# One pool of two-bank tiles for both phases of a hash-attention and gated feed-forward kernel

## The chip, the core and the metric

The kernel runs on one core of a Trainium2 chip. Its time is the device time in microseconds of one execution. Before the change, three runs gave a median of 914.16 us (913.9 to 914.45).

The engines are named as in the profile: PE multiplies matrices, DVE does elementwise work on vectors, ACT applies functions (exponential, sign, copy), POOL and SP mostly issue transfers. PE writes its results into PSUM, which is used here as eight banks of 512 float32 values per partition. DVE and ACT read them from there.

## The reference: what is computed

```python
# q, k, v: (4, 8, 768, 64); proj: (64, 6)
q_bits = (q @ proj > 0); k_bits = (k @ proj > 0)        # 6 bits each
mask = bucket(q_bits)[:, None] == bucket(k_bits)[None, :]
scores = where(mask, q @ k.T / 8, -1e9)
attn = exp(scores - max) ; attn = attn / (attn.sum(-1) + 1e-09)
x = (attn @ v) as (3072 tokens, 512)
g = x @ w_gate                                           # w_gate, w_val: (512, 1536)
out = (g * sigmoid(g) * (x @ w_val)) @ w_out             # w_out: (1536, 512)
```

The inputs of the second half are float64 values that the kernel takes as pairs of words.

## The kernel before, in words

**Attention.** Heads are taken two at a time: 4 batches x 4 head pairs make 16 pairs, the outer loop from L625. In a pair, queries lie in two halves of 384 (`HQ`) and keys in six chunks of 128 (`NCH`), so a pair has 12 units, one per half and chunk.

For a unit, `products` (L517) takes two PSUM banks, one for each head, and multiplies the float32 scores into them. `mark` (L521) adds a second product, of hash bits in bfloat16, which pushes pairs of different buckets far down. Then ACT takes the exponential of each head's bank on its own, into the weights `A` (L524). `attend` (L531) multiplies the weights of a unit by v into a bank per half of the queries. ACT copies that bank to `xT` at the end of each half (L549), with a small step for `e` after the first half (L548). A pair's 12 units of scores come first and its 12 `attend` steps after them.

`front` (L415) prepares a pair: the transposes of q and k (on PE for the first pair, in `start_first`, L453, and on DVE for the others) and the hash products (`hash_blocks`, L420), which go to a bank of their own. ACT takes their signs (L428). For k, DVE spreads them over the rows (`spread_k`, L434). In the first pair the order is written out at L478 to L488: units 0 to 2 are multiplied, the signs of k and q by halves are taken in between, and the marks follow.

DVE adds up the weights (`add`, L553). `total` (L572) lets PE sum them over partitions into a bank, and ACT copies the sums' row to SBUF (L581). SP then sends the row on, DVE inverts it (`invert`, L586), and `norm` (L600) scales `xT` one pair later. Inside the pair loop the order is: scores of 12 units, `total` of the pair before, the next pair's hash products (`prepare_pair`, L642), pieces of weights, `attend`.

All PSUM tiles of this phase come from one pool of eight single banks (L304). A new tile takes the slot that is released first, and waits for the last reader of what was in it.

**The gated block.** It opens a pool of four tiles of two banks each (L676), once the attention's pool is closed. Tokens are taken in three blocks of 1024. For each group of 128 hidden columns, `up` (L689) makes the gate and the value, each as a product `a` of two parts of a split number and a product `n` of a third part. ACT and DVE join them into `hid`, whose third part comes last (L742). After each three groups an output part follows (L749): eight chunks of 128 tokens, a two-bank tile each, the first bank with the products of the parts h and l (`first` in `start`, L755), the second bank with those of the third part (`second`). In the last part of each block, four chunks are begun ahead with the groups that are ready (`ahead`, L797). DVE adds a finished tile to the output (`end`, L773, with L785 and L789, or L777 ahead of L785).

The very last chunk (`last`, L800) uses two tiles: one for the third part's product, one whose two banks take the two halves of the output columns. After each half DVE adds it (L813) and SP sends it out (L816).

**Loads.** The first q goes out from SP and the first k from ACT (L350), each in two halves of chunks. The first v follows on SP (L353). Later SP gets k, q and v of the second pair (L408) and the first weight words. The SP queue is worked in order.

Every instruction waits for its inputs and for the release of the tile it writes. There is no scheduler: the order on each engine is the program's own.

## Time and profile before

| what | value |
|---|---|
| median of three runs | 914.16 us |
| the profiled execution, whole | 914.08 us |
| its span, first to last instruction | 912.0 us |
| PE busy | 904.2 us, 99% of the span |
| DVE busy | 667.2 us, 73% |
| ACT busy | 453.8 us, 50% |
| granted TensorE clock | 0.999 |
| `A<-sc` on ACT (L524), 128x384, 384 of them | 155.9 us |
| one head pair in full swing | 19.23 us |

The span is a little shorter than the device time, since something lies around it on both sides. A row of the profile names the line, the engine, the operation and its tiles (`out<-in`), then the number of instructions. The times are busy time, the mean of one, and the idle time of the engine just before. The busy share of PE says only that some matmul was running; where PE stood still is told by its waits.

### The profile page before, as it was taken

What the parts mean: (1) busy time and instruction counts of PE and PEld (TensorE: products, weight loads), DVE (VectorE), ACT (ScalarE), POOL (GpSimd) and SP (SyncE); (2) the same over time, 40 slices, a digit from 0 to 9 for tenths busy, and PEclk for the clock granted to TensorE, in tenths of its full rate; (3) what the DMA queues carried; (4) which work ended last, traced back from release to release, by engine and by line L of the source; (5) the groups of instructions that cost most, each with busy time, mean ns of one, the idle gap of its engine ahead of it and who ended that gap; (6) DMA issues with size and microseconds to landing.
All of it is one profiled execution on the core that took longest, in us unless ns stands there. A gap on an engine that the chain in (4) does not pass through costs nothing.

```text
span 912.0 us, 12995 instructions
## 1 busy us (share of the span) xinstructions
PE 904.2 (99%) x4795; PEld 638.8 (70%) x4795; DVE 667.2 (73%) x774; ACT 453.8 (50%) x812; POOL 97.0 (11%) x193
## 2 busy tenths in 40 slices
PE   9999999999999999999999999999999999999997
PEld 5444444444444488888888788888888888888886
DVE  5999999998989768679776756464658754574746
ACT  6889888788887655452414133322313233313230
POOL 1011101010111210001000000101010100010000
PEclk9999999999999999999999999999999999999999
DMA  8677797778886699686756563434444642525232
GB/s 185 127 199 204 212 210 174 173 209 233 216 192 208 209 374 334 224 283 208 279 198 235 206 232 104 181 132 173 138 148 152 239 157 99 185 73 210 99 138 93
DMA packets 145582, 174.28 MB, mean 191 GB/s; under 512 B 106496, under 2 KB 115200, under 8 KB 145520
## 3 DMA queue, kind: packets, MB, share of 16 engines
q0 software_dynamic: 22864, 116.36, 36.4%
q1 hardware_dynamic: 121056, 56.71, 24.8%
q8 instruction: 38, 0.62, 0.3%
q10 hardware_dynamic: 1600, 0.39, 0.2%
q14 instruction: 24, 0.20, 0.1%
HBM read 133.17 MB, written 39.42 MB: 189 GB/s over the span
## 4 chain that ended last, share of the span: by engine, by line
PE 97%; DVE 2%; DMA 0%; ACTq 0%; ACT 0%; issue 0%; DVEq 0%
PE a L687 29%; PE o L687 20%; PE sc L514 17%; PE n L687 14%; PE av L539 14%; PE sum L578 1%; PE hps L423 1%; DMA kraw<-in_k_dram 0%; DVE hid L742 0%; DVE hid L740 0%; DVE v L732 0%; DVE v L736 0%; DVE xparts L292 0%; ACTq L329 0%; ACT hid L737 0%
## 5 line engine op out<-in xcount | busy, mean ns | idle before, releaser
L687 PE MATMUL a<-xparts,ring 128*128 128x512 f32 x1152 | 273.0, 389 | 0.6 <-ACT row L581 0.6
L687 PEld LDWEIGHTS a<-xparts,ring 128*128 128x128 f32 x1152 | 216.2, 188 | 46.2 <-ACT row L581 1.3
L687 PE MATMUL o<-ring,hid 128*128 128x512 f32 (+1 forms) x870 | 199.0, 388 | 2.3 <-DVE o L813 1.2
L687 PEld LDWEIGHTS o<-ring,hid 128*128 128x128 f32 x870 | 162.5, 188 | 37.2 <-DVE hid L742 2.4
L524 ACT ACTIVATE A<-sc 128x384 f32<-128x384 f32 x384 | 155.9, 504 | 8.1 <-PE sc L514 7.3
L514 PE MATMUL sc<-qT,kT 64*128 64x384 f32 x768 | 157.5, 488 | 0.0
L687 PE MATMUL n<-xparts,ring 128*128 128x512 f32 x576 | 142.3, 389 | 0.0
L539 PE MATMUL av<-A,vraw 128*64 128x386 f32 (+1 forms) x768 | 127.7, 488 | 0.0
L687 PEld LDWEIGHTS n<-xparts,ring 128*128 128x128 f32 x576 | 108.1, 188 | 22.4
L732 DVE TENSOR_TENSOR v<-v,n 128x1024 f32<-128x1024 f32 x36 | 44.0, 1221 | 99.4 <-PE n L687 98.8
L244 POOL DMA_DIRECT2D ring<-ram x108 | 56.9, 529 | 501.2 <-PE n L687 329.2
L539 PEld LDWEIGHTS av<-A,vraw 128*64 128x64 f32 x768 | 53.7, 137 | 73.3 <-issue 61.4
L514 PEld LDWEIGHTS sc<-qT,kT 64*128 64x128 f32 x768 | 70.3, 187 | 47.8 <-issue 41.9
L726 ACT ACTIVATE g<-a 128x1024 f32<-128x1024 f32 x36 | 36.9, 1026 | 132.1 <-PE a L687 127.2
L737 ACT ACTIVATE hid<-v 128x1024 fp32r<-128x1024 f32 x36 | 38.2, 1062 | 114.8 <-DVE v L736 114.8
L734 ACT ACTIVATE g<-g 128x1024 f32<-128x1024 f32 x36 | 38.2, 1061 | 85.2 <-DVE g L732 85.2
L789 DVE TENSOR_TENSOR o<-o 128x512 f32<-128x512 f32 x92 | 63.0, 687 | 20.6 <-ACT o L783 18.2
L732 DVE TENSOR_TENSOR g<-g,n 128x1024 f32<-128x1024 f32 x36 | 43.8, 1216 | 33.3 <-PE n L687 33.3
L514 PE MATMUL sc<-qb,kb 64*128 64x384 bf16 x384 | 66.0, 323 | 0.0
L560 DVE SCALAR_TENSOR_TENSOR both<-A 128x1536 f32<-128x1536 f32 x32 | 55.8, 1744 | 7.4 <-ACT A L524 6.1
L564 DVE TENSOR_TENSOR both<-both,A 128x1536 f32<-128x1536 f32 x32 | 56.2, 1757 | 3.2
L740 DVE SCALAR_TENSOR_TENSOR hid<-hid,v 128x1024 fp32r<-128x1024 f32 x36 | 44.0, 1223 | 19.2 <-ACT hid L737 19.1
(79 smaller groups left out, 701.0 us busy)
## 6 DMA issues: line engine op xcount, KB each, us to landing
ring<-ram POOLq DMA_DIRECT2D x108, 768.0 KB, 4.8
ram<-stage POOLq DMA_DIRECT2D x23, 768.0 KB, 5.6
ram<-stage SPq DMA_DIRECT2D x13, 768.0 KB
qraw<-in_q_dram SPq DMA_DIRECT2D x64, 96.0 KB
vraw<-in_v_dram SPq DMA_DIRECT2D x16, 384.0 KB
out_dram<-o SPq DMA_DIRECT2D x23, 256.0 KB
kraw<-in_k_dram SPq DMA_DIRECT2D x60, 96.0 KB
r<-sums SPq DMA_DIRECT2D x30, 192.0 KB
```

The lines of the kernel that those rows point to most:

```text
L244: nc.gpsimd.dma_start(t.bitcast(FP32), ram[at].bitcast(FP32))
L514: nc.tensor.matmul(banks_of[u][h], x["k", n][rows, ks], x["q", n][rows, qs], start=start, stop=not start)
L524: nc.scalar.activation(weights(u)[:, h, 0:HQ], sc, AF.Exp, scale=SCALE * (1.0 if units[u][0] else OFF / 2))
L539: nc.tensor.matmul(ps[h * D : (h + 1) * D, 0:width], raws["v", n][:, h, c, :], a[:, h, 0:width], start=c == 0, stop=c == NCH - 1)
L560: nc.vector.scalar_tensor_tensor(out=t, in0=first, scalar=S * EPS / P / 2, in1=now, op0=ALU.add, op1=ALU.add)
L564: nc.vector.tensor_tensor(t, t, now, op=ALU.add)
L687: nc.tensor.matmul(ps, w, x, start=start, stop=stop)
L732: nc.vector.tensor_tensor(two(z), two(z), n_, op=ALU.subtract)
L734: nc.scalar.activation(z, z, AF.Silu)
L737: nc.scalar.activation(h, val, AF.Copy, scale=TOWARD / STEP)
L740: nc.vector.scalar_tensor_tensor(out=l, in0=h.bitcast(FP32), scalar=-STEP, in1=val, op0=ALU.mult, op1=ALU.add)
L789: nc.vector.tensor_tensor(accs[c], accs[c], t[:, 1], op=ALU.subtract)
```

## The change

The change does five things.

1. One pool `pp` of four two-bank tiles is opened at the start and serves both phases; the pool of single banks and the second pool go. A unit's two heads share one tile, and one exponential of 128x2x384 takes both. Both halves of `attend` share a tile; `e` and one copy of 128x768 come at the end of the pair. The nine warm-up products go to one tile, and each first transpose takes one bank of a two-bank tile.
2. The hash products of pair n+1 and the sums of pair n-1 share a tile, `joint`. Its sums' row is copied after the hash products have been issued and after the two signs of q on ACT: `total` now returns the copying step as a function.
3. In the first pair the order of signs and marks changes: two signs, products 1 and 2, and then mark 0, sign of k's second half, mark 1, sign of q's second half, mark 2.
4. The first v is loaded after k and q of the second pair.
5. In the last output part of a block, the last group's first products of chunks 0 and 1 both come before the second product of chunk 0. The very last chunk takes three tiles, one for each half and one for the third part.

The diff, cut to its core:

```diff
--- before.py
+++ after.py
@@ -75,7 +75,11 @@
     RINGS = (3, 3)
     ringp = [ctx.enter_context(tc.tile_pool(name="ringp", bufs=RINGS[0]))]
     dram = ctx.enter_context(tc.tile_pool(name="dram", bufs=1, space=bass.MemoryType.DRAM))
+    pp = ctx.enter_context(tc.tile_pool(name="pp", bufs=4, space=PSUM))
     ctx.enter_context(tc.manual_schedule())
+
+    def two_banks(name):
+        return pp.tile([P, 2, 512], FP32, tag="pp", name=name)
 
     halves = [slice(half * HQ, (half + 1) * HQ) for half in range(2)]
 
@@ -301,10 +305,6 @@
         fixed = scope.enter_context(tc.tile_pool(name="fixed", bufs=1))
         att = scope.enter_context(tc.tile_pool(name="att", bufs=2))
         xp = scope.enter_context(tc.tile_pool(name="xp", bufs=4))
-        banks = scope.enter_context(tc.tile_pool(name="ps", bufs=8, space=PSUM))
-
-        def bank(name):
-            return banks.tile([P, 512], FP32, tag="ps", name=name)
 
         pairs = [(b, pr) for b in range(B) for pr in range(NP)]
         raws = {}
@@ -350,7 +350,6 @@
         for half in range(2):
             fetch(0, "q", nc.sync, half)
             fetch(0, "k", nc.scalar, half)
-        fetch(0, "v", nc.sync)
 
         ident = fixed.tile([P, P], FP32, tag="ident", name="ident")
         make_identity(nc, ident)
@@ -363,9 +362,9 @@
         nc.vector.memset(zeros, 0.0)
         for t in (sides["k", 0], sides["q", 0], sides["q", 1]):
             nc.vector.memset(t, 0.0)
-        for _ in range(9):
-            ps = bank("idle")
-            nc.tensor.matmul(ps, zeros[:, 0:P], zeros[:, 0:512], start=True, stop=True)
+        idle = two_banks("idle")
+        for i in range(9):
+            nc.tensor.matmul(idle[:, i % 2], zeros[:, 0:P], zeros[:, 0:512], start=True, stop=True)
 
         HR = 16
         assert 2 * NBITS <= HR and 2 * HR == BLOCK
@@ -405,12 +404,20 @@
             twos.append(t)
         ring = [t[:, i] for t in twos for i in range(2)]
 
-        for name in "kqv":
-            fetch(1, name, nc.sync)
+        for n, name in ((1, "k"), (1, "q"), (0, "v"), (1, "v")):
+            fetch(n, name, nc.sync)
         load_words(3, nc.sync)
 
         T = {}
         bits = {}
+
+        joints = {}
+
+        def joint(n):
+
+            if n not in joints:
+                joints[n] = two_banks("joint")
+            return joints[n]
 
         def front(n):
             bits["q", n] = sides["q", n % 2]
@@ -418,7 +425,7 @@
             low, high = slice(0, BLOCK), slice(D, D + BLOCK)
 
             def hash_blocks(todo):
-                tile_ = bank("hps")
+                tile_ = joint(n - 2)[:, 1]
                 for i, (name, half) in enumerate(todo):
                     nc.tensor.matmul(tile_[i * BLOCK : (i + 1) * BLOCK, 0:HQ], hash_w,
                                      T[name, n][:, half * HQ : (half + 1) * HQ],
@@ -456,7 +463,7 @@
                     for name in "kq":
                         if not half:
                             T[name, n] = opnd.tile([P, S], FP32, tag=name + "T", name=name + "T")
-                        ps = bank("tps")
+                        ps = two_banks("tps")[:, 0]
                         for i in range(CH):
                             nc.tensor.transpose(ps[:, i * P : (i + 1) * P],
                                                 raws[name, n][:, half * CH + i].rearrange("p h d -> p (h d)"),
@@ -478,14 +485,14 @@
                 products(0)
                 todo = [("k", 0), ("q", 0), ("k", 1), ("q", 1)]
                 signs = hash_blocks(todo)
-                for i in range(3):
+                for i in range(2):
                     both_heads(signs[i], *todo[i])
                 products(1)
                 products(2)
-                mark(0)
-                both_heads(signs[3], *todo[3])
-                mark(1)
-                mark(2)
+                for i in range(3):
+                    mark(i)
+                    if i < 2:
+                        both_heads(signs[2 + i], *todo[2 + i])
 
             order = [("q", 0), ("q", 1), ("k", 0), ("k", 1)]
             if n:
@@ -511,18 +518,17 @@
             ks = slice(c * P, (c + 1) * P)
             for h in range(2):
                 rows = slice(h * D, (h + 1) * D)
-                nc.tensor.matmul(banks_of[u][h], x["k", n][rows, ks], x["q", n][rows, qs],
+                nc.tensor.matmul(banks_of[u][:, h], x["k", n][rows, ks], x["q", n][rows, qs],
                                  start=start, stop=not start)
 
         def products(u):
-            banks_of[u] = [bank("sc")[:, 0:HQ] for _ in range(2)]
+            banks_of[u] = two_banks("sc")[:, :, 0:HQ]
             product(u, T, True)
 
         def mark(u):
             product(u, bits, False)
-            for h, sc in enumerate(banks_of.pop(u)):
-                nc.scalar.activation(weights(u)[:, h, 0:HQ], sc, AF.Exp,
-                                     scale=SCALE * (1.0 if units[u][0] else OFF / 2))
+            nc.scalar.activation(weights(u)[:, :, 0:HQ], banks_of.pop(u), AF.Exp,
+                                 scale=SCALE * (1.0 if units[u][0] else OFF / 2))
 
         def score(u):
             products(u)
@@ -531,22 +537,19 @@
         def attend(u):
             n, half, c = units[u]
             a = weights(u)
-            if c == 0:
-                av[n] = bank("av")
-            ps = av[n]
+            if (half, c) == (0, 0):
+                av[n] = two_banks("av")
+            ps = av[n][:, half]
             width = AW if half == 0 else HQ
             for h in range(2):
                 nc.tensor.matmul(ps[h * D : (h + 1) * D, 0:width], raws["v", n][:, h, c, :],
                                  a[:, h, 0:width], start=c == 0, stop=c == NCH - 1)
-            if c == NCH - 1:
-                if half == 0:
-                    if n == len(pairs) - 1:
-                        xT[n] = lastp.tile([P, S], FP32, tag="last", name="lastx")
-                    else:
-                        xT[n] = xp.tile([P, S], FP32, tag="xT", name="xT")
-                    mean[n] = small.tile([P, 1], FP32, tag="e", name="e")
-                    nc.scalar.activation(mean[n], ps[:, HQ : HQ + 1], AF.Copy, scale=EPS)
-                nc.scalar.copy(xT[n][:, half * HQ : (half + 1) * HQ], ps[:, 0:HQ])
+            if (half, c) == (1, NCH - 1):
+                pool, tag = (xp, "xT") if n < len(pairs) - 1 else (lastp, "last")
+                xT[n] = pool.tile([P, S], FP32, tag=tag, name=tag)
+                mean[n] = small.tile([P, 1], FP32, tag="e", name="e")
+                nc.scalar.activation(mean[n], av[n][:, 0, HQ : HQ + 1], AF.Copy, scale=EPS)
+                nc.scalar.copy(xT[n].rearrange("p (x q) -> p x q", x=2), av[n][:, :, 0:HQ])
 
         both = {}
 
@@ -570,18 +573,22 @@
         sums = [dram.tile([P, each], FP32, tag=f"sums{i}", name="sums") for i in range(2)]
 
         def total(n):
-            ps = bank("sum")
+            ps = joint(n)[:, 0]
             t = [acc.pop((n, half)) for half in range(2)]
             for h in range(2):
                 for half in range(2):
                     g = (2 * h + half) * BLOCK
                     nc.tensor.matmul(ps[g : g + BLOCK, 0:HQ], ones, t[half][:, h, :],
                                      start=True, stop=True)
-            row = att.tile([P, HQ], FP32, tag="row", name="row", bufs=1)
-            nc.scalar.copy(row, ps[:, 0:HQ])
-            few = small.tile([P, each], FP32, tag="few", name="few")
-            nc.sync.dma_start(few, row.rearrange("(g r) t -> r g t", r=BLOCK)[0])
-            waiting.append(lambda: invert(n, few))
+
+            def fetch_row():
+                row = att.tile([P, HQ], FP32, tag="row", name="row", bufs=1)
+                nc.scalar.copy(row, ps[:, 0:HQ])
+                few = small.tile([P, each], FP32, tag="few", name="few")
+                nc.sync.dma_start(few, row.rearrange("(g r) t -> r g t", r=BLOCK)[0])
+                waiting.append(lambda: invert(n, few))
+
+            return fetch_row
 
         def invert(n, few):
             nc.vector.reciprocal(few, few)
@@ -637,10 +644,11 @@
                     add(u + i)
                 if i == (2 if n else TURN):
                     load(n + 2, "qk")
-            if n:
-                total(n - 1)
+            row = total(n - 1) if n else None
             if more:
                 prepare_pair(1)
+            if row:
+                row()
             finish(rest)
             finish(last)
             while waiting:
@@ -655,7 +663,7 @@
             advance_pieces()
             if n >= len(pairs) - 3:
                 bring()
-        total(len(pairs) - 1)
+        total(len(pairs) - 1)()
         finish(last)
         left.extend(waiting)
 
@@ -673,11 +681,6 @@
         hidp = scope.enter_context(tc.tile_pool(name="hidp", bufs=4))
         outp = scope.enter_context(tc.tile_pool(name="outp", bufs=1))
         homes.append(outp)
-        pp = scope.enter_context(tc.tile_pool(name="pp", bufs=4, space=PSUM))
-
-        def two_banks(name):
-            return pp.tile([P, 2, 512], FP32, tag="pp", name=name)
-
         hids = {}
         accs = {}
         rows = [out[b * S : (b + 1) * S, :].rearrange("(p c) m -> p c m", c=NCH) for b in range(B)]
@@ -752,7 +755,7 @@
                 hs = [hids[NQ * n + j] for j in range(NQ)]
                 tiles = {}
 
-                def start(c, js):
+                def start(c, js, steps=None):
                     if c not in tiles:
                         tiles[c] = two_banks("o")
                     t = tiles[c]
@@ -767,8 +770,8 @@
                         for j in js:
                             mm(t[:, 1], hs[j][:, 2, cols], ws[j][:, 2], j == 0, j == NQ - 1)
 
-                    for go in (second, first) if final and c >= ahead else (first, second):
-                        go()
+                    for go in steps or ("ba" if final and c >= ahead else "ab"):
+                        (first if go == "a" else second)()
 
                 def end(c):
                     t = tiles.pop(c)
@@ -798,19 +801,19 @@
                 for c in range(ahead):
                     yield lambda c=c: start(c, range(NQ - 1))
                 def last(c):
-                    t, tn = two_banks("o"), two_banks("o")
+                    tn, *ts = (two_banks("o")[:, 0] for _ in range(3))
                     cols = slice(c * P, (c + 1) * P)
                     for j in range(NQ):
-                        mm(tn[:, 0], hs[j][:, 2, cols], ws[j][:, 2], j == 0, j == NQ - 1)
-                    nc.vector.tensor_tensor(accs[c], accs[c], tn[:, 0], op=ALU.subtract)
+                        mm(tn, hs[j][:, 2, cols], ws[j][:, 2], j == 0, j == NQ - 1)
+                    nc.vector.tensor_tensor(accs[c], accs[c], tn, op=ALU.subtract)
                     batch, at = divmod(b * NCB + c, NCH)
                     for half in range(2):
                         here = slice(half * DM // 2, (half + 1) * DM // 2)
                         for j in range(NQ):
                             for v in range(2):
-                                mm(t[:, half, 0 : DM // 2], hs[j][:, v, cols], ws[j][:, v, here],
+                                mm(ts[half][:, 0 : DM // 2], hs[j][:, v, cols], ws[j][:, v, here],
                                    j == 0 and v == 0, j == NQ - 1 and v == 1)
-                        nc.vector.scalar_tensor_tensor(out=accs[c][:, here], in0=t[:, half, 0 : DM // 2],
+                        nc.vector.scalar_tensor_tensor(out=accs[c][:, here], in0=ts[half][:, 0 : DM // 2],
                                                        scalar=STEP + 1, in1=accs[c][:, here],
                                                        op0=ALU.mult, op1=ALU.add)
                         nc.sync.dma_start(rows[batch][:, at, here], accs[c][:, here])
@@ -821,7 +824,14 @@
                         return
 
                     def chunk(c=c):
-                        start(c, [NQ - 1] if c < ahead else range(NQ))
+                        if c >= ahead:
+                            start(c, range(NQ))
+                        elif c == 0:
+                            start(0, [NQ - 1], "a")
+                            start(1, [NQ - 1], "a")
+                            start(0, [NQ - 1], "b")
+                        else:
+                            start(c, [NQ - 1], "b" if c == 1 else "ab")
                         end(c)
                     yield chunk
 
```

## The prediction

> **What bounds the kernel now.** I read the page first, then the list of who waited for whom on PE, then the chain of work that ended last, and last the timeline of the few places where that chain leaves PE.
>
> ```profile
> PE 904.2 (99%) x4795; PEld 638.8 (70%) x4795; DVE 667.2 (73%) x774; ACT 453.8 (50%) x812; POOL 97.0 (11%) x193
> ...
> PE 97%; DVE 2%; DMA 0%; ACTq 0%; ACT 0%; issue 0%; DVEq 0%
> ```
>
> PE is busy 904.2 of 912.0 us, and 97% of the chain is PE. A faster ACT or DVE is therefore worth nothing by itself; only places where PE stands still can give time. The change takes no matmul away. The PE waits are all of these:
>
> ```profile
> PE idle L368 <- DVE kb L363: 1.3, 1, 1.3
> PE o L687 <- DVE o L813: 1.2, 1, 1.2
> PE o L687 <- DVE hid L742: 1.1, 3, 0.4
> PE a L687 <- ACT row L581: 0.6, 1, 0.6
> PE tps L461 <- DMA kraw<-in_k_dram: 0.3, 1, 0.3
> ```
>
> (Columns: us in all, times, longest.) The first is the start, which the change leaves. The other four add to 3.2 us, 0.35% of the run: this is nearly all that can be won. In the windows of the 16 head pairs, every full pair after the first takes 19.23 us with PE busy throughout, whatever DVE (16.9 to 18.5 us busy) and ACT (15.5 to 17.8) do.
>
> The sum is made against the profiled execution, 914.08 us: a span of 912.0 and 2.1 around it. The median of the three runs is 914.16, so 0.08 is added at the end.
>
> **Attention to gated block.** The chain from 300 to 330 us:
>
> ```profile
> 315.91 0.83 PE sum L578 x8
> ...
> 316.81 0.49 ACT row L581
> ...
> 317.34 3.94 PE a L687 x16
> ```
>
> The first product of the gated block waits until ACT has copied the last sums, because the old pool's banks must be free. With one pool for both phases its tile is the one of the last score unit, read long before (the built program's order shows no wait on ACT left there). The sum matmuls start at 315.84; in a full pair 16 such records (sums and hashes) fill 37.94 to 39.37, so 8 need 0.72, and `a` could begin at 316.56 instead of 317.34: gain 0.78 (0.6 by the wait row alone, 1.0 if the weight load ahead of `a`, idle 1.34, is also hidden).
>
> **The last chunk.** The timeline of the last 6 us:
>
> ```profile
> 907.31 0.42 DVE L813 SCALAR_TENSOR_TENSOR o<-o 128x256 f32<-128x256 f32 x1
> ...
> 907.79 0.98 PE L687 MATMUL o<-ring,hid 128*128 128x256 f32 x6 [1.24 <-DVE o L813]
> 908.81 0.42 DVE L813 SCALAR_TENSOR_TENSOR o<-o 128x256 f32<-128x256 f32 x1 [1.07 <-PE o L687]
> ```
>
> Both halves share a tile, so the second half's matmuls start only when DVE has read the first. With a tile each they follow the first half's (ended 906.55) and are done near 907.5. DVE then runs its two steps behind each other. Its rows just before start 0.61 apart, or 0.72 where a step needs the one before, at 0.69 each, so 0.34 to 0.45 at 0.42: the second starts near 907.75 instead of 908.81, gain 1.06 (0.9 to 1.1). The third tile waits for the sixth chunk's last step, done at 905.04 and wanted near 906.5. What is late next is DVE itself, which is back to back from 897.01; so nothing that PE gains just before counts here.
>
> **The end of each block's output part.** Three times PE waits for `hid` of the last hidden group:
>
> ```profile
> 502.16 1.24 DVE hid L742
> ...
> 503.44 10.76 PE o L687 x46
> ```
>
> `n` ended at 497.19 and `o` at 514.20: 17.01 us for 72 matmuls that take 16.32 in the other parts, so 0.69 is lost (0.64 in the second block). The change puts two matmuls of chunk 1 (2 x 0.227) ahead of the one that needs L742. The wait of 0.37 is thus covered. But a new one comes: chunk 4 needs chunk 0's tile, and DVE starts on chunk 0 only once that same matmul is done (now 503.98, then two steps of 0.7, released near 505.46). PE reaches chunk 4 after 8 more matmuls, at 503.44 + 8 x 0.227 = 505.25, instead of after 10. It restarts at 505.46 with 36 matmuls (8.16) and the restart cost seen in the row above (10.76 less 46 x 0.227 = 0.33), and ends at 513.95: gain 0.25, or 0.1 if chunk 0 comes 0.1 later. I take 0.2, twice: 0.4 (0.1 to 1.2). In the last block DVE sets the end, and nothing is gained here.
>
> **Values loaded later.** q goes out from SP and k from ACT by 2.9 us, and v follows on SP at 3.72. The windows of half a microsecond show 1.18 MB moved by 7.0 us, which is q, k and v together; q and k alone (786 KB) had passed by 5.35 in bytes. k's second half landed at 6.57, and PE waited 0.30 for it. Without v it should land near 5.6, and the transposes run on at their pace of 0.36 per three: 6.14 instead of 6.70. Behind that stand the qT copy on DVE (free at 7.00 after its first half), the first scores and the hash products, which then begin at 7.88 instead of 8.32: gain 0.44 (0 if k is late for another reason). On SP, v of pair 0 now stands behind the eight loads of pair 1, near 12.5 instead of 3.72; the weight words behind it shift by the 393 KB (1.1 us at the 350 GB/s of 15 to 20 us). v is needed at 20.1 and should land before 17; words are needed at 23.05. Without that cover the whole lateness would fall on PE.
>
> **The first pair.** ACT's order changes here:
>
> ```profile
> 10.49 0.57 ACT L428 ACTIVATE kb<-hps,columns 32x384 bf16<-32x384 f32 x1
> 11.09 0.87 ACT L524 ACTIVATE A<-sc 128x384 f32<-128x384 f32 x2
> 11.98 0.58 ACT L428 ACTIVATE qb<-hps,columns 32x384 bf16<-32x384 f32 x1
> 12.59 2.79 ACT L524 ACTIVATE A<-sc 128x384 f32<-128x384 f32 x7
> ```
>
> Now the exponential of unit 0 comes before the third sign, that of unit 1 before the fourth. No row shows an exponential of 768. From 384 (491 ns) and the gate's 1024 from PSUM (1026) I get 0.81 by the line between them, and 0.87 from the row of two halves; I take 0.82, nearer the single instruction. Without the clock shift above: both heads' marks are done at 11.21, unit 0's exponential runs to 12.08, the third sign to 12.67, its spread on DVE (0.66) to 13.34. Unit 3's marks need that spread: they start at 13.4 instead of 11.9. Unit 4 needs unit 1's tile (exponential done 13.52). From there PE is at its own 0.807 per unit: the eleventh unit's last mark starts near 19.9 instead of 19.11. Loss 0.75 (0.3 if the signs overlap more, 1.1 if the exponentials do not overlap at all). Queued behind the waiting marks on PE are all later units and the hashes of pair 1.
>
> The Trainium skill speaks against this twice. "Perfetto Trace Analysis", section "Matmul Optimizations", wants all eight PSUM banks in use; here transposes and warm-up products take one bank of a two-bank tile. By the rows only this start pays. The same page, section "Optimizing Scalar/DVE Operations", says to break instructions up where ACT is not saturated yet makes bubbles elsewhere, and this change joins them. If that held in every pair, a tile held 0.43 longer (the second head's share) with no slack would cost 12 x 0.43 per pair, 77 us in 15 pairs. The row says otherwise: in a full pair a unit's exponential ends about 0.85 after its marks, and its tile is wanted three units, 2.4 us, after. The sum takes 0.
>
> **The other pairs.** One exponential per unit takes some 0.07 off ACT per unit; not on the path. The copy of `av`, one of 768 at the end, ends near 1.05 after the last attend product, by its wanted use 2.45 after (third unit later): ACT waited for PE at this copy in all 15 pairs, so slack is 1.4. The sums' row, copied behind two signs, comes some 1.75 later, so its DMA on SP and DVE's reciprocal (wait now 8.3 in 10 pairs) come up to 1.7 later. Behind it on DVE are splits and weight pieces, then the next transposes, with 6 us to spare before the hash products. Taken as 0; from -0.5 (fewer waits on PE) to +0.5.
>
> **Sum.** 0.78 + 1.06 + 0.4 + 0.44 - 0.75 = 1.93. 914.08 - 1.93 + 0.08 = 912.2.
>
> **Rivals.**
> Given back at the start: k does not land earlier (0 instead of 0.44), the first pair loses 1.1, and the blocks give 0.1. Then 0.6 + 1.06 + 0.1 - 1.1 = 0.66, 913.5; as not all of it need come together, 913.0 is its centre. For it: the new ACT order is certain. Against: PE's wait on k is in the list.
> Everything shown goes: DVE's chunk 0 is no obstacle, 0.69 + 0.64 from the blocks, 1.0 at the boundary, the first pair loses 0.3: 1.0 + 1.06 + 1.33 + 0.44 - 0.3 = 3.5, 910.6; for a part of it 911.2. Against: the tile of chunk 4 is wanted too early.
> Slower: the fourth unit of every pair waits for the one copy of `av`. It decides when ACT is over 1.4 us late at the last attend product. At 0.3 per pair, 15 x 0.3 = 4.5 less the 1.9: 916.8. Against: ACT stood idle before that copy in every pair.
>
> **Chances.** Forecast 55% (912.2, own range 911.7 to 912.7), given back 30% (913.0), everything goes 10% (911.2), slower 5% (916.8). 0.2% of the time, 1.8 us, is about what a measurement can tell from no change: the line lies at 912.3, inside the forecast's own range. About 0.7 of the forecast, 0.15 of the second case and all of the third lie beyond it: 0.385 + 0.045 + 0.10 = 0.53 faster; 0.05 slower; the other 0.42 within. The range 911.3 to 913.5 leaves out the slower case and the far ends of the second and third, some 0.15 in all.
>
> **What would show it.** Right: PE's waits on L742, on the row copy, on DVE's first half step and on k are gone; the second half step follows the first by 0.4 to 0.5; full pairs still take 19.23; the first pair's attend begins some 0.3 later than 20.14. A PE wait on DVE `o` in the fourth chunk of each block's last part shows the new gate. Wrong: a pair length other than 19.23, above all one with PE waiting for ACT's copy; or a first pair that is not later, which would mean that my order of signs and exponentials is not what holds PE.

## The result and the profile after

The changed kernel took 912.32 us in the median of 22 executions (911.99 to 913.91), the kernel before, beside it, 914.34 (22 executions, 913.75 to 916.19). The ratio is 0.9976, 95% interval 0.997 to 0.9983. The execution that was profiled took 913.47 us (span 911.4), 1.15 above the median. So its trace also holds something that the typical execution does not hold in full, and this turned out to be the part of the change that the prediction had put at nothing.

Busy shares and chain of the page after:

```profile
PE 904.0 (99%) x4795; PEld 636.1 (70%) x4795; DVE 666.6 (73%) x774; ACT 448.0 (49%) x604; POOL 97.0 (11%) x193
...
PE 97%; DVE 1%; DMA 1%; ACTq 0%; issue 0%; ACT 0%; DVEq 0%
```

PE's busy time is the same and ACT has 208 instructions less. In the chain DMA has 1% where it had 0, DVE 1% where it had 2. PE's waits after (us in all, times, longest):

```profile
PE idle L367 <- DVE kb L362: 1.3, 1, 1.3
PE sc L521 <- DVE kb L444: 1.1, 2, 0.7
PE tps L468 <- DMA kraw<-in_k_dram: 0.6, 1, 0.6
PE sc L521 <- ACT A L530: 0.6, 1, 0.6
```

The waits on DVE's first half step, on `hid` and on the row copy are gone. Two are new: for the spread of k (`kb`; 0.38 of it in the first pair, 0.73 in the sixth) and for the exponential. The wait for the first k is still there. The chain at the boundary, at the end of the first block, and DVE's timeline at the very end:

```profile
317.78 0.78 PE joint L581 x8
318.56 3.89 PE a L690 x16
```

```profile
496.54 1.81 PE n L690 x8
498.35 16.71 PE o L690 x72
```

```profile
906.91 0.68 DVE L808 TENSOR_TENSOR o<-o 128x512 f32<-128x512 f32 x1
907.69 0.76 DVE L816 SCALAR_TENSOR_TENSOR o<-o 128x256 f32<-128x256 f32 x2
```

From the sums to `a` it is 0.78 instead of 1.43; `o` of the first block takes 16.71 instead of 17.01, that of the second 16.76 instead of 16.96; both half steps of the last chunk lie within 0.76. ACT in the first pair:

```profile
9.82 0.57 ACT L435 ACTIVATE qb<-joint,columns 32x384 bf16<-32x384 f32 x1
11.17 0.81 ACT L530 ACTIVATE A<-sc 128x768 f32<-128x768 f32 x1 [0.78 <-PE sc L521]
12.01 0.58 ACT L435 ACTIVATE kb<-joint,columns 32x384 bf16<-32x384 f32 x1
12.61 0.81 ACT L530 ACTIVATE A<-sc 128x768 f32<-128x768 f32 x1
```

Between 9.82 and 11.17 ACT stands idle for 0.78 us: the third sign could run there, but stands behind an exponential whose marks are not done. Unit 3's marks then wait on PE until 13.33, and `attend` begins at 20.92 instead of 20.14.

The rest of the difference shows when the `attend` starts of the 16 pairs are read off PE's timeline and subtracted. Before, every pair took 19.22 to 19.24 (the last, without a next pair, 18.58). After, the fourth to sixth distances are 19.33, 20.14 and 19.30: 1.08 in all. Two windows of 19.23 us, from the `attend` start of the first and of the fifth pair on (columns: us, busy time of PE, PEld, DVE, ACT, POOL, then clock, DMA share and GB/s):

```profile
20.92:40.15 19.23, 19.23 (x141) 9.20 (x137) 17.70 (x19) 15.13 (x23) 2.07 (x3) 1.00 0.87 158
...
97.94:117.17 19.23, 18.50 (x132) 9.25 (x132) 18.50 (x24) 15.74 (x25) 2.38 (x4) 1.00 0.78 176
```

In the first PE is busy throughout, and the window ends where the next `attend` starts. In the second PE lacks 0.73, the wait for `kb` in the list above, and the next `attend` starts only at 118.08. The other 0.35 of the 1.08 stands in no row of waits. The spans add up: start +0.08, first pair -0.86, standstills -1.08, boundary +0.65, blocks +0.30 and +0.20, last part +1.23, together +0.52 against a measured 0.6.

### The profile page after: what moved, and what is told of

It reads as the page before. It is cut to its first block, busy times and chain, and to the rows that moved or that the text cites. A ratio compares the mean times of both kernels' runs of the same rounds, so it can differ in the third digit from the quotient of the medians.

```text
span 911.4 us, 12610 instructions
## 1 busy us (share of the span) xinstructions
PE 904.0 (99%) x4795; PEld 636.1 (70%) x4795; DVE 666.6 (73%) x774; ACT 448.0 (49%) x604; POOL 97.0 (11%) x193
## 4 chain that ended last, share of the span: by engine, by line
PE 97%; DVE 1%; DMA 1%; ACTq 0%; issue 0%; ACT 0%; DVEq 0%
PE a L690 29%; PE o L690 22%; PE sc L521 17%; PE n L690 14%; PE av L545 13%; PE joint L581 1%; PE joint L430 1%; DMA vraw<-in_v_dram 1%; DMA kraw<-in_k_dram 0%; DVE both L567 0%; DVE both L563 0%; DVE acc L570 0%; ACTq L329 0%; DVE kb L444 0%; DVE kT L458 0%
## 5 line engine op out<-in xcount | busy, mean ns | idle before, releaser
L530 ACT ACTIVATE A<-sc 128x768 f32<-128x768 f32 x192 | 151.8, 815 | 7.5 <-PE sc L521 4.2
L521 PEld LDWEIGHTS sc<-qT,kT 64*128 64x128 f32 x768 | 67.6, 187 | 48.5 <-issue 46.3
L521 PE MATMUL sc<-qb,kb 64*128 64x384 bf16 x384 | 63.4, 323 | 1.1 <-DVE kb L444 1.1
```

Source lines behind the costliest of these rows:

```text
L521: nc.tensor.matmul(banks_of[u][:, h], x["k", n][rows, ks], x["q", n][rows, qs], start=start, stop=not start)
L530: nc.scalar.activation(weights(u)[:, :, 0:HQ], banks_of.pop(u), AF.Exp, scale=SCALE * (1.0 if units[u][0] else OFF / 2))
```

## The theory and its rivals

**Theory.** (a) The late first pair comes from ACT's order, not from the joined exponential. (b) The standstills come from copying the sums' row behind two signs. The row's transfer, into the small tile `few`, then stands on SP behind the eight loads of q and k; these wait for DVE's transposes, as the raw tiles have one buffer; DVE is in order, so the reciprocal that waits for the row holds up the next transposes, and these the next loads. The trace shows each link. SP's queue after, its wait for DVE in all 14 rounds first:

```profile
SPq L337 <- DVE qT L458: 46.1, 14, 5.9
...
61.45 2.77 SPq L337 DMA_DIRECT2D kraw<-in_k_dram  x4
64.31 0.60 SPq L588 DMA_DIRECT2D few<-row  x1
```

and DVE after, with its wait in all:

```profile
DVE few L594 <- DMA few<-row: 12.7, 10, 2.8
...
66.51 0.23 DVE L594 RECIPROCAL few<-few 128x12 f32<-128x12 f32 x1 [1.79 <-DMA few<-row]
...
73.04 0.97 DVE L458 STREAM_TRANSPOSE kT<-kraw 128x768 f32<-128x768 f32 x1
```

DVE's wait for `few` is 12.7 us in ten pairs, 8.3 before; but it differs from one execution to the next (10.0 in run 1, and 5.2 and 12.2 in runs 7 and 8, which leave before's attention part as it was), so these two figures alone prove nothing. (c) k's landing does not depend on v.

**Rivals.** The joined exponential frees tiles late; DVE is simply full in the pairs with two weight pieces; late v and weight words feed the standstill; v delays k, as the prediction had it. Twelve runs tested these. They were made in three groups, each with its own runs of the kernel before beside it (medians 913.97, 914.13 and 914.15 us, so 0.2 between runs of different groups says little). "Attend" below is the start of the first pair's.

## Experiments

**1. The changed kernel again** (`after_again`), nothing edited.

> The changed kernel once more, nothing edited. Its profiled execution of 913.47 us held a standstill of PE of 0.73 us in the sixth pair (PE waiting for DVE's spread of k), while most of its executions took 912.0 to 912.8. Theory: the standstill is not in every execution; in this profile PE's wait for the spread of k in the sixth pair is under 0.3 us if the profiled execution is near 912.3, and again near 0.7 if it is near 913.4. Rival: it is in every execution, whatever the time, and the longer times come from elsewhere. The first pair's attend should begin at 20.9 to 21.0 in any case, and sums-to-gate, blocks and last chunk should repeat 0.78, 16.7 and 20.5 us (n's end to span's end).

Measured: 912.94 us (21 executions, 912.18 to 914.62), ratio 0.9988 (0.9982 to 0.9995). The profiled execution, 913.91, has distances of 20.06 and 20.13 in the fifth and sixth place, 1.73 us of standstill; 913.91 - 1.73 = 912.18 is just the quickest execution. For the first profile, 913.47 - 1.08 = 912.39. So the changed kernel takes about 912.2 when PE never stands, and its median depends on how often it does. The boundary (0.78) repeats; attend begins at 20.75, a little earlier than expected.

**2. Old order of signs in the first pair** (`old_signs`):

```diff
-for i in range(2): both_heads(signs[i], *todo[i])
+for i in range(3): both_heads(signs[i], *todo[i])
 products(1); products(2)
-for i in range(3):
-    mark(i)
-    if i < 2: both_heads(signs[2 + i], *todo[2 + i])
+mark(0); both_heads(signs[3], *todo[3]); mark(1); mark(2)
```

> The changed kernel with the order of before in the first pair (three signs, then the first marks, then the fourth sign). Theory: the first pair loses 0.78 us in the change because the first exponential of 768 goes ahead of k's second sign and so delays the marks of unit 3. With the old order the marks of unit 3 start near 12.6 instead of 13.33, attend begins near 20.2 instead of 20.95, and the run is 0.7 to 0.8 us shorter than the changed kernel. Rival: the loss comes from the joined exponential, which frees a score tile later whatever the order; then attend begins at 20.7 or later and the gain is 0.25 or less.

Measured: 912.16 us (911.48 to 912.86), ratio 0.9979 (0.997 to 0.9988), 0.78 under run 1. ACT:

```profile
10.38 0.57 ACT L435 ACTIVATE kb<-joint,columns 32x384 bf16<-32x384 f32 x1
11.14 0.81 ACT L530 ACTIVATE A<-sc 128x768 f32<-128x768 f32 x1 [0.18 <-PE sc L521]
```

The third sign fills the gap, the exponential starts no later (11.14), unit 3's marks start at 12.75, attend at 20.25. The standstill is 0.31 here, so part of the 0.78 may be standstill; the traces give the order's share without it. Counted from the first hash product, attend begins 11.82 later in the kernel before (and in runs 7 to 10, within 0.01), 12.67 in the changed kernel (12.66 to 12.67 in the five other profiles with the new order and joined exponentials), and 12.04 here and in run 12. Of the 0.85 that the first pair loses, the order makes 0.63. So (a) holds for the larger part only: 0.22 stays with the joined tiles and exponentials, which no run here takes apart. Unit 3's products still wait 0.58 for unit 0's exponential and start 3.80 after the first hash product, where it was 2.91 before.

**3. v of the first pair early again** (`v_early`):

```diff
     fetch(0, "k", nc.scalar, half)
+fetch(0, "v", nc.sync)
...
-for n, name in ((1, "k"), (1, "q"), (0, "v"), (1, "v")):
+for n, name in ((1, "k"), (1, "q"), (1, "v")):
```

> The changed kernel with v of the first pair loaded where it was before (behind q, ahead of k and q of the second pair). Theory: k's second half lands when its own chain of transfers is done, whatever v adds, so it lands at 6.5 to 6.6, the hash products begin at 8.25 to 8.35, and the time is that of the changed kernel within 0.15 us. Rival (the step of the prediction): v's 393 KB delay k; then k lands later than 6.9 or the hash products begin at 8.6 or later, and the run is 0.3 to 0.5 us longer. Second question: if the late v and the weight words behind it feed the standstill in the sixth pair, that wait (0.7 us in the changed kernel's profile) goes here.

Measured: 913.09 us (912.53 to 913.96), ratio 0.9989 (0.9982 to 0.9995): as run 1. Bytes in half microseconds show what k waits for. First the changed kernel, then this one (the last column is GB/s):

```profile
5.50:6.00 0.50, 0.48 (x5) 0.24 (x3) 0.17 (x1) 0.31 (x1) 0.00 (x0) 1.00 0.29 51
6.00:6.50 0.50, 0.00 (x0) 0.00 (x0) 0.48 (x1) 0.18 (x1) 0.00 (x0) 1.00 0.00 0
```

```profile
5.50:6.00 0.50, 0.21 (x2) 0.00 (x0) 0.16 (x1) 0.41 (x1) 0.00 (x0) 1.00 0.91 275
6.00:6.50 0.50, 0.00 (x0) 0.00 (x0) 0.47 (x2) 0.00 (x0) 0.00 (x0) 1.00 0.91 335
```

In both PE does nothing from 6.0 to 6.5, and the transposes of k's second half start at 6.62 and 6.54. Without v not a byte moves in that half microsecond, yet k is not there. ACT's queue carries nothing but this k, and its last packet ends at 5.85 in the changed kernel, 5.81 here and 5.73 in the kernel before: v takes nothing from k's transfer. What is waited for is the report of a transfer whose bytes are through. (c) holds: over all profiles the hash products begin at 8.24 in the mean of six with v early and at 8.23 in that of eight with v late. The Trainium skill has this cost for another way of issuing ("DMA: Bandwidth & Descriptors", section "Anatomy of one DMA — SWDGE (gpsimd) path"): some 2 us per transfer that do not depend on its size, most of it the wait for the receipt of the last byte. These three traces show 0.73 to 0.97 from k's last packet to PE's start. A sum by the bytes of q, k and v together gave 0.44 for v's removal; since k's packets end no earlier without v and the tail stays, it is 0, and 0.08 was measured between the first two profiles. In the profile the standstill was 0.24, in the median nothing came of it: late v and words do not feed it.

**4. Row copied right away** (`row_first`):

```diff
-row = total(n - 1) if n else None
+if n: total(n - 1)()
 if more: prepare_pair(1)
-if row: row()
```

> The changed kernel with the sums' row copied right after its products, ahead of the next pair's hash products in program order, as before. Theory: copying the row behind two signs puts its transfer and DVE's reciprocal 1.3 to 2.2 us later in each pair; behind the reciprocal DVE is in order, so the next transposes and k's spread come later, and the sixth pair has under 0.6 us to spare. Here the reciprocals come at the times of before counted from each pair's start (about 1.3 to 2 us earlier), PE's wait for k's spread in the sixth pair is 0 to 0.2, and the run is 0.3 to 0.8 us shorter than the changed kernel if most of its executions hold that wait, 0 if they don't. Rival: the copy ahead of the signs delays signs and spread by its 0.49 us, hash bits come later, and the run is the same or longer, up to 0.5 us.

Measured: 924.53 us, ratio 1.0114 (1.0098 to 1.0129). Both theories missed. PE's waits:

```profile
PE joint L430 <- ACT row L586: 9.5, 14, 0.8
```

The hash products write the second bank of `joint`, the row copy reads the first, but the wait is set for the tile: PE waits 0.67 for ACT in each of 14 pairs, and a pair takes 20.10 instead of 19.23; 14 x 0.87 = 12.2. The Trainium skill ("PSUM — Partial Sum Buffer", section "The four PSUM rules") calls each bank a separate memory; nothing in that asks for such a wait, and the row says that what counts here is which tile a bank belongs to. So the late copy is not a free choice of the change: with a shared tile, the early copy costs 12 us.

**5. Row's transfer from POOL's queue** (`row_pool`):

```diff
-nc.sync.dma_start(few, row...)
+nc.gpsimd.dma_start(few, row...)
```

> The changed kernel with one edit: the transfer of the sums' row to the small tile for the reciprocal goes out from POOL's queue instead of SP's, so that it no longer stands behind SP's eight loads of q and k. The copy of the row stays behind two signs. Theory: the standstills of 0.1 to 0.9 us in the fifth to seventh pair come from a loop (transposes on DVE, SP's loads that wait for them, the row's transfer behind these, the reciprocal that waits for it, the next transposes behind the reciprocal). Without SP in it the reciprocals come 2 us or more earlier, every pair from the second to the fifteenth takes 19.23, and the run is at 912.0 to 912.3, with no execution above 912.6: 0.7 us under the median of 912.94 that the changed kernel had on the same kind of comparison. Rival: DVE is simply full in the pairs with two pieces; then the standstills stay at 0.5 or more, and the median at 912.7 or more.

Measured: 912.27 us (912.23 to 912.68), ratio 0.9976 (0.9967 to 0.9986). All distances are 19.22 to 19.23. DVE:

```profile
DVE few L594 <- DMA few<-row: 5.4, 6, 1.7
```

One queue changed on a transfer of 6 KB and DVE's wait falls to 5.4 (it is 8.2 to 12.7 in the five profiles that copy the row as late and leave its transfer on SP and the weight pieces alone), PE's standstills go, and ten executions lie within 0.45 us, where the 21 of run 1 spread over 2.4. Two of the ten are at 912.66 and 912.68, just above the expected bound. DVE's work in the fifth pair is the same 18.50 us as in the window above, so DVE being full is not the cause by itself: it is full and waits besides.

**6. Two exponentials per unit** (`two_exps`):

```diff
-nc.scalar.activation(weights(u)[:, :, 0:HQ], banks_of.pop(u), AF.Exp, ...)
+sc = banks_of.pop(u)
+for h in range(2):
+    nc.scalar.activation(weights(u)[:, h, 0:HQ], sc[:, h], AF.Exp, ...)
```

> The changed kernel with two exponentials of 384 for each unit instead of one of 768; tiles and order stay. Theory: joined or not, ACT's exponential is off the path in full pairs (19.23 us, PE busy throughout); the pair lengths stay, ACT is about 10 to 15 us busier in all, and the run is that of the changed kernel within 0.3 us. In the first pair each unit's two exponentials end near 0.9 us after the start of the first instead of 0.82, so that attend begins up to 0.1 later. Rival (the rule that instructions are to be broken up where ACT makes bubbles elsewhere): the first head's exponential starts one product earlier, so PE's wait of 0.6 for the exponential in the first pair shrinks by 0.3 or more, and attend begins 0.2 or more earlier.

Measured: 913.50 us (912.80 to 914.68), ratio 0.9993 (0.9986 to 0.9999). Attend 21.00, PE's wait for the exponential still 0.6: the rival for the first pair falls (12.79 from the first hash product, later than the 12.67 of one exponential). The median was 0.56 above run 1's, more than the 0.3 expected; the runs of before beside it were 0.16 higher too. The profile, 913.33, has 0.86 of standstill, all in the fifth and sixth place; the other pairs are 19.23. So splitting brings nothing in full pairs. Whether the extra ACT instructions make the standstill more frequent is not shown.

**7. Before, last chunk in three tiles only** (`before_last3`):

```diff
-t, tn = two_banks("o"), two_banks("o")
+tn, *ts = (two_banks("o")[:, 0] for _ in range(3))
...
-mm(t[:, half, 0 : DM // 2], ...)
+mm(ts[half][:, 0 : DM // 2], ...)
```

> The kernel before with nothing but the last chunk's three tiles. Theory: the second half's products no longer wait for DVE's first half step, the second half step follows the first within 0.35 to 0.5, and the run is 1.06 to 1.25 us shorter than before (the changed kernel's profile has 20.54 us from the end of the last n to the end of the span, against 21.76). Rival: the output's transfers or SP's issue set the end; then less than 0.6 is gained.

Measured: 913.26 us (912.91 to 915.65) against 914.13, ratio 0.9991 (0.9983 to 0.9999). The two half steps lie within 0.76 (907.12 on), and from the start of the last `o` (889.87) to the end of the span it is 20.93, against 21.94 before (890.06 to 912.0): 1.01. The fastest executions differ by 0.94. Slightly under the expectation, because the 1.22 read from the changed kernel held another part (run 8).

**8. Before, new order of the last group's products only** (`before_aab`):

```diff
-start(c, [NQ - 1] if c < ahead else range(NQ))
+if c >= ahead: start(c, range(NQ))
+elif c == 0: start(0, [NQ - 1], "a"); start(1, [NQ - 1], "a"); start(0, [NQ - 1], "b")
+else: start(c, [NQ - 1], "b" if c == 1 else "ab")
```

> The kernel before with nothing but the new order of the last group's products for chunks 0 and 1 in each block's last part. Theory: 0.3 and 0.2 us from the first two blocks, 0 from the last, where DVE sets the end: 0.4 to 0.5 shorter than before; PE's waits for hid L742 (1.1 us in all) are gone, and in their place the fourth begun chunk's tile is a gate that only the weight loads wait for. Rival: chunk 4's wait for chunk 0's tile takes all of it back; then PE shows a wait for DVE's step on o of 0.3 or more in each block and the run is within 0.15 of before.

Measured: 913.33 us (913.07 to 916.02), ratio 0.9994 (0.9986 to 1.0003), 0.80 under the median and 0.78 under the fastest of before. `o` takes 16.72 and 16.74 in the first two blocks. The surplus is in the last block. There, before, the prediction called DVE back to back; it was not:

```profile
904.35 0.69 DVE L785 SCALAR_TENSOR_TENSOR o<-o 128x512 f32<-128x512 f32 x1
905.20 0.69 DVE L777 TENSOR_TENSOR o<-o 128x512 f32<-128x512 f32 x1 [0.16 <-PE o L687]
```

With the new order the same pair of rows:

```profile
905.61 0.69 DVE L785 SCALAR_TENSOR_TENSOR o<-o 128x512 f32<-128x512 f32 x1
906.22 0.69 DVE L777 TENSOR_TENSOR o<-o 128x512 f32<-128x512 f32 x1
```

0.61 apart instead of 0.85: the 0.24 that PE gained ahead of the last chunk but one did count. 0.29 + 0.22 + 0.24 = 0.75.

This profile (915.11 us) also held a standstill of 1.90 us in the fourth to sixth distance, though its attention part is that of before. So the standstill needs neither the late copy nor joined tiles; before's own tail (up to 916) is likely the same thing, only rarer, and run 10 tests it.

**9. Before, row copied late only** (`before_row_late`), tiles as before:

```diff
-if n: total(n - 1)
+row = total(n - 1) if n else None
 if more: prepare_pair(1)
+if row: row()
```

(`total` returns its copying step here too.)

> The kernel before with nothing but the late copy of the sums' row (behind the hash products and two signs), its tiles as they were. Theory: this is the part of the change that lets the standstills in: the reciprocals come 1.3 to 2 us later, PE waits for the spread of k in the fifth to seventh pair by 0.7 to 1.8 us in all in most executions, and the median is 0.5 to 1.2 us above before. Rival: the standstills come from the later first pair or from the joined tiles; then all pairs are 19.23 and the median is within 0.2 of before.

Measured: 915.53 us (914.00 to 916.54) against 914.15, 1.4 above in the median; the ratio, 1.0007 (0.9999 to 1.0015), leaves the size open. Eight of 13 executions are above 915 (of before's 34, five). In the profile (914.52) the fifth and sixth distance hold 0.54, and DVE's wait for `few` is 9.6. The late copy alone makes the standstill frequent; joined tiles and a late first pair are not needed for that.

**10. Before, row's transfer from POOL's queue only** (`before_row_pool`), the edit of run 5 in the kernel before.

> The kernel before with nothing but the row's transfer on POOL's queue. Theory: before has the same loop with only 0.3 us to spare, and its executions above 914.5 (up to 916.1) are those in which it stands still. Here all pairs are 19.23, the median is within 0.15 of before's fast executions (913.8 to 914.0), and none is above 914.5. Rival: before's slow tail comes from elsewhere, and executions at 915 and above remain.

Measured: 913.66 us (913.45 to 913.94, 21 executions), ratio 0.9993 (0.9986 to 0.9999). The tail is gone, and DVE's wait for `few` is 0.3 (5.2 to 12.2 in the three profiles with before's attention part): the tail came from this loop. The 0.3 below before's fast executions lie outside the span (913.70 less 911.9 is 1.8 in this kernel, where it is 2.1 in before); the spans agree.

**11. Weight pieces spread evenly** (`pace_even`):

```diff
-PACE = [2] * 4 + [1] * 4 + [2, 1] * 4
+PACE = [1, 2] * 8
```

> The changed kernel with the weight pieces spread evenly over the pairs (1, 2, 1, 2, ... instead of 2, 2, 2, 2, 1, 1, 1, 1, then 2, 1 in turn). Theory: the loop of transposes, loads, row's transfer and reciprocal takes over 19.23 only in the pairs with two pieces, so that four of them in a row use up what is to spare. With pieces in turn the reciprocals keep their place from pair to pair, all pairs take 19.23, and the run is at 912.0 to 912.4. Rival: the loop is long by itself, whatever the pieces; then a standstill of 0.5 or more stays in the fifth to seventh pair.

Measured: 911.90 us (911.70 to 912.77), ratio 0.9973 (0.9961 to 0.9984); 0.3 of it is again outside the span (1.8). All distances 19.22 to 19.23. With the pieces in turn the spread begins at most 6.24 after an attend start, so even with the late row over 1 us is to spare. Four pairs in a row with two pieces bring the loop near its limit; the late row makes the standstill frequent, but, as run 8 shows, is not needed for one.

**12. Both edits that gained** (`old_signs_row_pool`): runs 2 and 5 together.

> The changed kernel with both edits that gained by themselves: the order of signs of before in the first pair, and the row's transfer from POOL's queue. Theory: the two are apart in place and add up. Attend of the first pair begins near 20.2, pairs two to fifteen take 19.23 each, no wait of PE for the spread of k, and the run is at 911.3 to 911.7, a spread of executions under 0.6: 0.6 to 0.9 under the version with the row's transfer alone (912.27). Rival: with the first pair shorter everything on DVE and SP is due earlier, and a standstill of 0.3 or more comes back in the fifth to seventh pair; then 911.9 or more.

Measured: 911.62 us (911.50 to 912.12, five executions), ratio 0.9968 (0.9955 to 0.998). Attend 20.15, all distances 19.22 to 19.23, PE's only waits are the start's, k's (0.7) and one exponential's (0.6). Its span, 909.4, is the shortest of all the profiles. It was not run beside the changed kernel itself; the intervals of the ratios overlap, but the 0.63 of the first pair's order (12.04 from the first hash product instead of 12.67) is seen in the traces.

**How close the loop was.** From the attend start of the fifth pair to the start of the spread of k on DVE, and what the distance after it was over 19.23:

| run | to the spread, us | standstill, us |
|---|---|---|
| pace_even | 5.12 | 0 |
| before_last3 | 6.49 | 0 |
| before_row_pool | 6.49 | 0 |
| old_signs_row_pool | 6.96 | 0 |
| row_pool | 7.00 | 0 |
| before | 7.31 | 0 |
| v_early | 7.53 | 0 |
| old_signs | 7.83 | 0.18 |
| before_row_late | 8.11 | 0.46 |
| after_again | 8.30 | 0.83 |
| two_exps | 8.43 | 0.78 |
| before_aab | 8.47 | 0.94 |
| after | 8.56 | 0.91 |

PE stands once the spread begins later than about 7.6. Three of these profiles have before's attention part unchanged: `before` has 0.3 us to spare, `before_last3` 1.1, and `before_aab` is 0.9 too late. So what is to spare changes by up to 2 us from one execution to the next; what changes it no run shows.

## Why the prediction was right, and where it was not

The time (912.2 against 912.32) was right, and so was the direction of every part but v's, which gave nothing; some sizes were off and made up for each other. That the median came within 0.12 is partly luck: it depends on how often PE stands, and in run 1 the same kernel had 912.94 and only 1.03 less than before, where 1.93 was forecast. By the fastest executions the gain is 1.76 and 1.49, near the 1.60 of the parts below.

- **Boundary**, "0.78": 0.65 in the profile. By the chain, `a` follows the start of the sums after 0.78; the forecast of 316.56 meant 0.65 after the chain's 315.91. The eight records were taken a little too short.
- **Last chunk**, "1.06": 1.01 alone (run 7). Right in mechanism and size; the half steps are 0.34 apart where 0.34 to 0.45 was said.
- **Block ends**, "0.4": 0.30 + 0.20 in the first two blocks, and 0.24 in the last, where the prediction said nothing would be gained. The failed claim is that DVE is "back to back from 897.01": a row of the same timeline has a wait of 0.16 for PE, so PE was on the path there. The foreseen gate on chunk 4's tile is there, but only the weight loads wait for it (0.3 at each block), so PE lost nothing.
- **Values later**, "0.44": 0.08. The step that failed is "Without v it should land near 5.6": the bytes of all queues were added up as if v delayed k, and were taken for the landing. k's own packets end at 5.73 with v and at 5.85 without, and PE starts 0.97 and 0.77 later (run 3). The zero end ("0 if k is late for another reason") was the true one.
- **First pair**, "0.75": 0.85 from the first hash product, of which the order makes 0.63 and the joining 0.22 (run 2). The exponential of 768 took 0.815 against 0.82, and unit 3's marks started at 13.33 against 13.4. With the start this made attend 0.78 later where 0.3 was forecast.
- **Other pairs**, "0": the mechanism was named (the row 1.75 later, the reciprocal up to 1.7), but the cover was misjudged: "with 6 us to spare" was counted from the transposes of one pair to its hash products. It leaves out that the row's transfer stands behind loads that wait for those transposes, so that a delay comes back in the next pair, and that the spread of k, not the hash products, is wanted first. To spare were 0.3 us in that execution. The price is 1.08 and 1.73 in the two profiles; by the medians less 912.2, the time without it, it is typically 0.1 in the first comparison and 0.7 in run 1. By the prediction's own sign, a pair length other than 19.23, it was wrong here: three pairs took 19.33, 20.14 and 19.30.

Without standstill the parts give 0.08 - 0.86 + 0.65 + 0.50 + 1.23 = 1.60, and 914.08 - 1.60 = 912.48 for the profiled kernel, 0.3 above what was forecast. The rival that the one copy of `av` would hold every pair was rightly put low: no list of PE's waits has such a row. Of the two rules weighed, neither decided: two-bank tiles cost nothing at the transposes, and breaking the exponentials up gained nothing (run 6). What the tiles did cost is 0.22 in the first pair and the shared `joint`, which ties the copy to a late place.

## What to carry to other kernels

When a step is moved later on one engine, follow its transfer into its queue and see what it now stands behind; if that waits for an engine which in turn waits for the step, the delay comes back each round and eats what is to spare within a few rounds, although every single round looks covered. Two purposes in one tile shared one wait here, although they used different banks. Where an engine sets the end, read every row of it for idle time before calling it full.

## What was not expected of the hardware

- PE could start on k only 0.73 to 0.97 us after the last packet of its 96 KB transfers, and 393 KB more on another queue did not move that packet: 5.73 and 5.81 us with them, 5.85 without (run 3).
- Whether the loop stands is decided anew in each execution: the same kernel took 912.18 and 914.62 us, and with one small transfer moved to another queue ten executions lay within 0.45. What differs between executions is open.
- The time outside the span differs between kernels, 1.8 or 2.1 us, and is steady in each; differences of 0.3 are therefore read from spans.
